# Narrower score products in a gated linear attention with a PReLU network: 80 and 112 columns instead of 128 and 116

## The chip, the cores and the metric

The kernel runs on one core of one Trainium2 chip. The metric is the device time of one execution in microseconds (us), the median of several runs; lower is better. A core has a matrix engine (TensorE, PE in the profile, with its weight loads shown apart as PEld), VectorE (DVE), ScalarE (ACT), GpSimd (POOL) and SyncE (SP), which here only issues DMAs. They run at the same time and wait for each other by semaphores. TensorE reads SBUF and writes PSUM; VectorE and ScalarE read both.

## The reference

Four sequences of 768 tokens, 8 heads of 48 channels, all in float32. Each head keeps a 48 x 48 state that is multiplied by a gate f, one value per channel, and takes in one outer product per token:

```python
f = 1.0 / (1.0 + np.exp(-f_logit))
for t in range(S):
    state = f[:, :, t, :, None] * state + np.einsum('bhd,bhe->bhde', k[:, :, t], v[:, :, t])
    y[:, :, t] = np.einsum('bhd,bhde->bhe', q[:, :, t], state)
```

The result goes as x, 3072 tokens of 384 channels, through a network with 2048 hidden channels and a slope per channel below zero:

```python
h = x @ w_in
g = np.maximum(h, 0.0) + alpha * np.minimum(h, 0.0)
return g @ w_out
```

## The kernel before

Tokens go in chunks of C = 128. A step handles U = 2 sequences of one chunk, so there are 12 steps. Heads lie in pairs, one at partitions 0 to 47 and one at 64 to 111 (`par`), four pairs to a sequence (`HP`). Inside a chunk the recurrence is a masked product of scores: token t takes from token s the sum over channels of q[t] times k[s] times all the gates after s up to t. The 128 x 128 scores are built from blocks of DB = 32 tokens, and each diagonal block from quads of 4 tokens (NB = 8 quads to a block). Inside a quad the gates between s and t are few, and they are multiplied into q: `qd` holds q with the products of d gates, for d = 0 to 3. Between quads the kernel multiplies k by the gates to the end of its quad (`k4`), and q by the gates from the beginning of its own quad and of the m - 1 quads between (`us`).

Preparing a step (VectorE and ScalarE; cut). W is 1024 tokens' columns (2 sequences x 4 pairs x 128), G = 32 blocks:

```python
qd = const.tile([128, 4 * (W + 1)], F32, tag="qd", name="qd")
for d in range(1, 4):                       # what no lag reaches is zeroed once
    nc.gpsimd.memset(qd[:, d * W:(d + 1) * W].rearrange("p (n r) -> p n r", r=4)[:, :, 0:d], 0.0)
# ... per step:
nc.scalar.activation(f, f, AF.Sigmoid)
nc.scalar.copy(kr[:, :, 2:3], f[:, :, 3:4])
qdv = [qd[:, d * W:(d + 1) * W] for d in range(4)]
nc.scalar.copy(qdv[0], q)
def lagged(d):
    nc.vector.tensor_tensor(quads(qdv[d])[:, :, d:4], quads(qdv[d - 1])[:, :, d:4],
                            f[:, :, 1:5 - d], ALU.mult)
# ... lagged(1), lagged(2), lagged(3) between products of f; then:
q4 = us[:, :, 0:DB].rearrange("p g (i r) -> p g i r", r=4)
skew = qd.rearrange("p (r x) -> p r x", r=4)[:, :, 0:W].rearrange("p r (n four) -> p n r four", four=4)
nc.scalar.copy(q4, skew[:, :, :, 0].rearrange("p (g i) r -> p g i r", i=NB))
# ... two scans, then q4 *= first gate of each quad, and us for the further quads: earlier(2) to earlier(7)
```

The gather takes row r of each quad from lag r, at a stride. The scores of one sequence (`attend`), two products and their evictions into the diagonal blocks `ad`:

```python
for u in range(U):
    raw = pair(f"raw{u}_{i}")               # one of 2 PSUM buffers of two banks
    for hp in range(HP):
        for j in range(NJ):
            g = (u * HP + hp) * C + j * DB
            for par in range(2):
                r_ = rows(par)
                nc.tensor.matmul(raw[DB * j:DB * (j + 1), par, hp * C:(hp + 1) * C],
                                 lhsT=k[r_, g:g + DB],
                                 rhs=qd[r_, 0:4 * W].rearrange("p (d x) -> p d x", d=4)[:, :, g:g + DB],
                                 start=True, stop=True)
    for d in range(4):
        nc.vector.copy_predicated(adu, mraw[:, d]..., rv[:, :, d])      # 128 x 256
    qu = pair(f"qu{u}_{i}")
    # the same loops: matmul(qu[..., hp * UW:(hp + 1) * UW], lhsT=k4[...], rhs=us[r_, g])   UW = 116
    for m in range(1, NB):
        nc.vector.copy_predicated(ad[:, u, :, :, 4 * m:DB], mquad..., qu...)   # 224, 192, ... 32
    yield
for u in range(U):
    # four ScalarE copies of ad into A
    yield
# py: the scores A (and the incoming state) times v; yield
# the state moved on (VectorE), y copied (ScalarE), xT[...] <- y by 10 DMAs; yield
```

So every 32 x 32 diagonal block is multiplied with all four lags: 4 x 32 = 128 columns. A float32 `matmul` shows as two MATMUL and two LDWEIGHTS records.

`carry` makes the products between blocks (`off`), a transpose (`pk`) and the new state (`pd`). `network` is the second half, in 12 pieces: eight of `ph` = x times w_in for two groups of 128 hidden channels, each with a ScalarE and two VectorE instructions that give `g`, and four of `po` = g times w_out. The pieces of neighbouring steps are interleaved by strings in which P and Q stand for pieces of prepare (of this and of the next step), O of carry, S of attend, n of the network of the step before, and a, w, b, v for pieces of loading the two weights, which are unpacked on the chip in the first steps:

```python
first = ("P3 a P a2 w P O a w3 S a P w S O a Q a S3 w a w S w Q a", ...)      # the first four steps
usual = "O n4 S n S Q n Q O n S2 n Q n Q S n S n Q n Q"
```

Each engine takes its instructions in the order in which the program issues them.

Of the kernel before, what the change touches and what calls it, by code (L numbers as in the profile page):

```python
# [8 lines left out]
F32 = mybir.dt.float32  # L9
# [3 lines left out]
I32 = mybir.dt.int32  # L13
U32 = mybir.dt.uint32
AF = mybir.ActivationFunctionType
ALU = mybir.AluOpType

C = 128
DB = 32
# [5 lines left out]
NB = DB // 4  # L25
# [5 lines left out]
def kernel(  # L31
# [28 lines left out]
    nc = tc.nc  # L60
    B, NC, _, HP, _ = qT.shape
    DM = v.shape[-1]
    H = 2 * HP
# [5 lines left out]
    W = U * HP * C  # L69
    GC = W // CH  # L70
    G = W // DB
    NJ = C // DB
    UO = [0, 0]
    for m in range(1, NB):
        UO.append(UO[-1] + (DB if m == 1 else DB - 4 * m))
    UW = UO.pop()

    const = ctx.enter_context(tc.tile_pool(name="const", bufs=1))
    work = ctx.enter_context(tc.tile_pool(name="work", bufs=2))
# [3 lines left out]
    def pair(name):  # L83
        return psa.tile([128, 2, 512], F32, tag="pair", name=name)
# [17 lines left out]
    ones = const.tile([128, NS], F32, tag="ones", name="ones")  # L102
    nc.gpsimd.memset(ones, 0.0)
    nc.gpsimd.memset(ones[:, 0:NS:NB + 1], 1.0)
    qd = const.tile([128, 4 * (W + 1)], F32, tag="qd", name="qd")
    for d in range(1, 4):
        nc.gpsimd.memset(qd[:, d * W:(d + 1) * W].rearrange("p (n r) -> p n r", r=4)[:, :, 0:d], 0.0)
    nc.gpsimd.memset(qd[:, 4 * W:], 0.0)
    bias = const.tile([128, 2], F32, tag="bias", name="bias")
    nc.gpsimd.memset(bias[:, 0:1], -896.0 * 128)  # L110
    nc.gpsimd.memset(bias[:, 1:2], -(896.0 + 2048) * 128)
# [2 lines left out]
    mraw = const.tile([128, 4, NB, 4], F32, tag="mraw", name="mraw")  # L114
# [5 lines left out]
    nc.vector.tensor_reduce(inq, diag, mybir.AxisListType.X, ALU.add)  # L120
    mquad = const.tile([128, UW], F32, tag="mquad", name="mquad")
    nc.gpsimd.memset(mquad, 0.0)
    for m in range(1, NB):
        lo = UO[m] + (4 if m == 1 else 0)
        n = NB - m
        nc.gpsimd.tensor_copy(mquad[:, lo:lo + 4 * n].rearrange("p (i r) -> p i r", r=4),
                              inq[:, 0:n].unsqueeze(2).broadcast_to((128, n, 4)))
    ad = const.tile([128, U, 2, HP, DB], F32, tag="ad", name="ad")
# [82 lines left out]
    def rows(par):  # L211
        return slice(64 * par, 64 * par + D)

    def quads(t):
        return t.rearrange("p (n r) -> p n r", r=4)
# [12 lines left out]
    def prepare(bp, c, x):  # L228

        i = f"{bp}_{c}"  # L230
# [3 lines left out]
        def load(name, src, bufs=2):  # L234
            t = work.tile([128, W], F32, tag=name, name=f"{name}_{i}", bufs=bufs)
            loads.dma_start(out=t.rearrange("p (u x) -> p u x", u=U),  # L236
                              in_=src[b0:b0 + U, c].rearrange("u p h t -> p u (h t)"))
            return t

        f = quads(load("f", fT, 1))  # L240
        q = load("q", qT, 1)
        k = x["k"] = load("k", kT, 1)
# [5 lines left out]

        nc.scalar.activation(f, f, AF.Sigmoid)
        nc.scalar.copy(kr[:, :, 2:3], f[:, :, 3:4])  # L250
        qdv = [qd[:, d * W:(d + 1) * W] for d in range(4)]
        nc.scalar.copy(qdv[0], q)  # L252
        fq = fs[:, 0:NS - 1].rearrange("p (g i) -> p g i", i=NB + 1)[:, :, 1:NB + 1]
        by32 = "p (g i) r -> p g (i r)"

        def lagged(d):
            nc.vector.tensor_tensor(quads(qdv[d])[:, :, d:4], quads(qdv[d - 1])[:, :, d:4],  # L257
                                    f[:, :, 1:5 - d], ALU.mult)

        nc.vector.tensor_tensor(kr[:, :, 1:2], f[:, :, 2:3], f[:, :, 3:4], ALU.mult)  # L260
        lagged(1)
        nc.vector.tensor_tensor(kr[:, :, 0:1], f[:, :, 1:2], kr[:, :, 1:2], ALU.mult)
        lagged(2)
        nc.vector.tensor_tensor(fq, f[:, :, 0:1].rearrange(by32, i=NB), kr[:, :, 0:1].rearrange(by32, i=NB), ALU.mult)
        lagged(3)
        yield

        ps = work.tile([128, NS], F32, tag="ps", name=f"ps_{i}", bufs=1)  # L270
        us = x["us"] = work.tile([128, G, UW], F32, tag="us", name=f"us_{i}", bufs=1)
        q4 = us[:, :, 0:DB].rearrange("p g (i r) -> p g i r", r=4)
        skew = qd.rearrange("p (r x) -> p r x", r=4)[:, :, 0:W].rearrange("p r (n four) -> p n r four", four=4)
        nc.scalar.copy(q4, skew[:, :, :, 0].rearrange("p (g i) r -> p g i r", i=NB))  # L274
        nc.vector.tensor_tensor_scan(ps, fs, ones, 0.0, ALU.mult, ALU.add)
        ss = work.tile([128, NS], F32, tag="ss", name=f"ss_{i}", bufs=1)
        nc.vector.tensor_tensor_scan(ss[:, ::-1], fs[:, ::-1], ones[:, ::-1], 0.0, ALU.mult, ALU.add)
# [15 lines left out]
        k4 = x["k4"] = work.tile([128, W], F32, tag="k4", name=f"k4_{i}", bufs=1)  # L293
# [108 lines left out]
    def attend(bp, c, x):  # L402

        i = f"{bp}_{c}"
        k, k4, us = (x[n] for n in ("k", "k4", "us"))


        for u in range(U):
            raw = pair(f"raw{u}_{i}")
            for hp in range(HP):  # L410
                for j in range(NJ):
                    g = (u * HP + hp) * C + j * DB
                    for par in range(2):
                        r_ = rows(par)
                        nc.tensor.matmul(raw[DB * j:DB * (j + 1), par, hp * C:(hp + 1) * C],  # L415
                                         lhsT=k[r_, g:g + DB],
                                         rhs=qd[r_, 0:4 * W].rearrange("p (d x) -> p d x", d=4)[:, :, g:g + DB],
                                         start=True, stop=True)
            adu = ad[:, u].rearrange("p r h t -> p (r h) t")
            rv = raw.rearrange("p r (h d t) -> p (r h) d t", h=HP, d=4)  # L420
            for d in range(4):
                nc.vector.copy_predicated(  # L422
                    adu, mraw[:, d].rearrange("p i r -> p (i r)").bitcast(I32).unsqueeze(1).broadcast_to((128, H, DB)),
                    rv[:, :, d])
            qu = pair(f"qu{u}_{i}")
            for hp in range(HP):
                for j in range(NJ):
                    g = (u * HP + hp) * NJ + j
                    for par in range(2):
                        r_ = rows(par)  # L430
                        nc.tensor.matmul(qu[DB * j:DB * (j + 1), par, hp * UW:(hp + 1) * UW],  # L431
                                         lhsT=k4[r_, g * DB:(g + 1) * DB], rhs=us[r_, g], start=True, stop=True)
            for m in range(1, NB):
                lo = UO[m] + (4 if m == 1 else 0)
                n = DB - 4 * m
                nc.vector.copy_predicated(  # L436
                    ad[:, u, :, :, 4 * m:DB],
                    mquad[:, lo:lo + n].bitcast(I32).unsqueeze(1).unsqueeze(1).broadcast_to((128, 2, HP, n)),
                    qu[:, :, 0:HP * UW].rearrange("p r (h x) -> p r h x", h=HP)[:, :, :, lo:lo + n])
# [4 lines that stand above are left out]
                s_ = slice(DB * j, DB * (j + 1))  # L444
                nc.scalar.copy(A[s_, u, :, s_], ad[s_, u].rearrange("p r h t -> p (r h) t"))  # L445
            yield


        py = pair(f"py_{i}")
        for u in range(U):  # L450
            for hp in range(HP):
                for cc in range(NC2):
                    for par in range(2):
                        hd = 2 * hp + par
                        o = hp * C + CH * cc
                        nc.tensor.matmul(py[64 * par:64 * par + 64, u, o:o + CH],  # L456
                                         lhsT=vs[bp][:, cc, u, hd * D:hd * D + 64],
                                         rhs=A[:, u, par * HP + hp, CH * cc:CH * (cc + 1)],
                                         start=True, stop=True)
        yield  # L460
        if c < NC - 1:
            x["moved"](1)
        y = work.tile([128, U, HP, C], F32, tag="ksn", name=f"y_{i}", bufs=1)
        for u in range(U):
            nc.scalar.copy(y[:, u].rearrange("p h t -> p (h t)"), py[:, u])
        xT = x["T"] = work.tile([128, NK, T], F32, tag="xT", name=f"xT_{i}")
        for hd in range(H):
            d = hd * D
            while d < (hd + 1) * D:
                n = min((hd + 1) * D, (d // 128 + 1) * 128) - d  # L470
                p0 = 64 * (hd % 2) + d - hd * D
                (nc.sync if hd % 2 else nc.scalar).dma_start(
                    out=xT[d % 128:d % 128 + n, d // 128].rearrange("p (u t) -> p u t", u=U),
                    in_=y[p0:p0 + n, :, hd // 2])
                d += n
        yield

    def network(bp, c, x):
# [37 lines left out]

    steps = [(bp, c) for c in range(NC) for bp in range(B // U)]
    first = (
# [4 lines left out]
    )  # L523
    usual = "O n4 S n S Q n Q O n S2 n Q n Q S n S n Q n Q"
    pieces = {key: part for keys, parts in (("aw", load_weights(w_in_sb, w_in, "w_in")),
                                            ("bv", load_weights(w_out_sb, w_out, "w_out")))
              for key, part in zip(keys, parts)}
# [74 lines left out]
```

## Time and profile before

| what | value |
|---|---|
| time, median of 3 runs | 670.87 us (670.18 to 671.96) |
| span of the profiled run | 670.8 us, 17033 instructions |
| mean granted TensorE clock | 0.994 |
| PE / PEld / DVE / ACT busy | 626.8 / 465.9 / 419.8 / 263.8 us |
| raw: PE busy, mean of one record | 29.4 us, 286 ns (1536 records) |
| qu: PE busy, mean of one record | 27.5 us, 274 ns (1536 records) |
| eviction of raw, DVE | 42.5 us, 443 ns (96) |
| gather into us, ACT | 24.7 us, 2059 ns (12) |

How to read it: a line of a group gives the line of the code, the engine, the operation, output <- inputs, shape and count; then the busy time, the mean time of one, and the idle time of the engine just before it, with what ended that. The chain of waits is followed back from the last instruction, at each step to what released it. Records of small matmuls overlap, so a group's busy time is less than count times mean.

### The profile page before, as it was taken

How to read it: one execution, taken by the hardware profiler on the slowest of the kernel's cores; microseconds unless marked ns; L12 is line 12 of the kernel's file. 1: busy time of each engine (PE TensorE's matmuls, PEld its weight loads, DVE VectorE, ACT ScalarE, POOL GpSimd, SP SyncE). 2: the span in 40 equal slices, each digit the busy share in tenths (PEclk: the TensorE clock that was granted, in tenths of full speed). 3: DMA queues.
4: the chain of work that ended last, by engine and by line, in shares of the span. 5: the costliest groups of instructions: out<-in, count | busy, mean ns of one | idle time of the engine just before them, and what ended most of it. 6: DMA issues, size and time to landing. Idle time of an engine off the chain costs nothing.

```text
span 670.8 us, 17033 instructions
## 1 busy us (share of the span) xinstructions
PE 626.8 (93%) x7392; PEld 465.9 (69%) x7392; DVE 419.8 (63%) x897; ACT 263.8 (39%) x457; POOL 70.8 (11%) x113
## 2 busy tenths in 40 slices
PE   0558899999999999999999999999999999999997
PEld 0446766876876876875876876876876786786774
DVE  5899889692675486486387397297298197170120
ACT  5755794443152441451450450451441442421110
POOL 8232232010000001001001001001001000000000
PEclk9998899999999999999999999999999999999999
DMA  6878996212112023023022023023023010000000
GB/s 230 268 199 273 264 247 166 60 40 69 34 64 72 3 64 87 18 64 79 26 64 79 25 65 79 24 64 79 25 64 80 25 34 24 24 3 24 24 0 23
DMA packets 29129, 53.03 MB, mean 79 GB/s; under 512 B 4320, under 2 KB 16864, under 8 KB 29056
## 3 DMA queue, kind: packets, MB, share of 16 engines
q0 software_dynamic: 9616, 27.92, 15.1%
q1 hardware_dynamic: 13584, 21.63, 10.3%
q10 hardware_dynamic: 5856, 2.40, 1.5%
q8 instruction: 58, 0.95, 0.6%
q14 instruction: 15, 0.12, 0.1%
HBM read 36.21 MB, written 4.72 MB: 61 GB/s over the span
## 4 chain that ended last, share of the span: by engine, by line
PE 82%; DVE 9%; ACT 3%; DMA 3%; issue 2%; ACTq 0%; DVEq 0%; SPq 0%
PE po L502 34%; PE ph L486 34%; PE py L456 4%; PE raw L415 3%; PE qu L431 3%; PE pk L368 2%; DVE ad L436 2%; DMA xT<-y 2%; PE pd L380 2%; DVE ad L422 2%; ACT us L274 1%; PE off L355 1%; DVE us L288 1%; DMA w_out_raw<-in_w_out 1%; DVE g L494 1%
## 5 line engine op out<-in xcount | busy, mean ns | idle before, releaser
L486 PE MATMUL ph<-xT,w_in_sb 128*128 128x256 f32 x1152 | 265.6, 388 | 7.5 <-DMA xT<-y 7.5
L502 PE MATMUL po<-w_out_sb,g 128*128 128x384 f32 x768 | 252.9, 488 | 0.2 <-DVE g L494 0.2
L486 PEld LDWEIGHTS ph<-xT,w_in_sb 128*128 128x128 f32 x1152 | 219.0, 193 | 42.5 <-DMA w_in_sb<-w_in_lead 6.9
L502 PEld LDWEIGHTS po<-w_out_sb,g 128*128 128x128 f32 x768 | 144.8, 190 | 97.7 <-ACT neg L491 0.8
L494 DVE SCALAR_TENSOR_TENSOR g<-neg,om,ph 128x256 f32<-128x256 f32 x192 | 83.3, 476 | 202.3 <-ACT neg L491 201.9
L491 ACT ACTIVATE neg<-ph 128x512 f32<-128x512 f32 x96 | 57.1, 597 | 140.4 <-PE ph L486 132.4
L508 ACT COPY o<-po 128x384 f32<-128x384 f32 x24 | 11.5, 479 | 156.7 <-PE po L502 156.7
L436 DVE COPY_PREDICATED ad<-mquad,qu 128x224 f32<-128x224 int32 (+6 forms) x168 | 50.4, 300 | 8.4 <-DVE ad L422 0.5
L288 DVE TENSOR_TENSOR us<-us,fs 128x768 f32<-128x768 f32 (+2 forms) x72 | 44.5, 617 | 0.2
L422 DVE COPY_PREDICATED ad<-mraw,raw 128x256 f32<-128x256 int32 x96 | 42.5, 443 | 2.7
L274 ACT COPY us<-qd 128x1024 f32<-128x1024 f32 x12 | 24.7, 2059 | 40.0 <-DVE qd L257 35.3
L445 ACT COPY A<-ad 32x256 f32<-32x256 f32 x96 | 38.4, 400 | 2.3 <-DVE ad L436 0.9
L236 POOL DMA_DIRECT2D k<-in_kT x11 | 8.0, 731 | 272.1 <-PE raw L415 239.2
L431 PE MATMUL qu<-us,k 48*32 48x116 f32 x1536 | 27.5, 274 | 5.2 <-DVE us L288 2.3
L339 ACT COPY A<-q 48x512 f32<-48x512 f32 x48 | 29.6, 617 | 5.7 <-DVE f L334 4.1
L415 PE MATMUL raw<-qd,k 48*32 48x128 f32 x1536 | 29.4, 286 | 2.4 <-DVE ad L422 2.4
L456 PEld LDWEIGHTS py<-A,vs 128*64 128x64 f32 x768 | 25.1, 145 | 7.2 <-ACT neg L491 3.3
L415 PEld LDWEIGHTS raw<-qd,k 48*32 48x32 f32 x1536 | 22.6, 110 | 10.4 <-issue 10.4
L355 PE MATMUL off<-q,kh 48*32 48x32 f32 x768 | 9.4, 199 | 20.7 <-DVE q L306 20.0
L257 DVE TENSOR_TENSOR qd<-qd,f 128x768 f32<-128x768 f32 (+2 forms) x36 | 27.1, 752 | 2.0 <-ACT qd L252 2.0
L431 PEld LDWEIGHTS qu<-us,k 48*32 48x32 f32 x1536 | 22.5, 109 | 8.3 <-PE raw L415 5.7
L456 PE MATMUL py<-A,vs 128*64 128x64 f32 x768 | 26.9, 231 | 0.9 <-DVE vs L396 0.7
(66 smaller groups left out, 442.5 us busy)
## 6 DMA issues: line engine op xcount, KB each, us to landing
w_in_raw<-in_w_in SPq DMA_DIRECT2D x12, 511.8 KB, 6.2
w_out_raw<-in_w_out SPq DMA_DIRECT2D x12, 511.8 KB, 5.3
f<-in_fT POOLq DMA_DIRECT2D x11, 512.0 KB, 4.4
q<-in_qT POOLq DMA_DIRECT2D x11, 512.0 KB, 5.1
k<-in_kT POOLq DMA_DIRECT2D x11, 512.0 KB, 4.0
out<-o SPq DMA_DIRECT2D x24, 192.0 KB, 1.9
vs<-in_v POOLq DMA_DIRECT2D x22, 192.0 KB, 4.6
w_in_sb<-w_in_lead POOLq DMA_DIRECT2D x12, 256.0 KB, 5.8
```

Source lines behind the costliest of these rows:

```text
L274: nc.scalar.copy(q4, skew[:, :, :, 0].rearrange("p (g i) r -> p g i r", i=NB))
L288: nc.vector.tensor_tensor(us[:, :, UO[m]:UO[m] + 4 * n].rearrange("p g (i r) -> p g i r", r=4), us[:, :, skip:skip + 4 * n].rearrange("p g ...
L415: nc.tensor.matmul(raw[DB * j:DB * (j + 1), par, hp * C:(hp + 1) * C], lhsT=k[r_, g:g + DB], rhs=qd[r_, 0:4 * W].rearrange("p (d x) -> p d ...
L422: nc.vector.copy_predicated(adu, mraw[:, d].rearrange("p i r -> p (i r)").bitcast(I32).unsqueeze(1).broadcast_to((128, H, DB)), rv[:, :, d])
L431: nc.tensor.matmul(qu[DB * j:DB * (j + 1), par, hp * UW:(hp + 1) * UW], lhsT=k4[r_, g * DB:(g + 1) * DB], rhs=us[r_, g], start=True, stop= ...
L436: nc.vector.copy_predicated(ad[:, u, :, :, 4 * m:DB], mquad[:, lo:lo + n].bitcast(I32).unsqueeze(1).unsqueeze(1).broadcast_to((128, 2, HP, ...
L445: nc.scalar.copy(A[s_, u, :, s_], ad[s_, u].rearrange("p r h t -> p (r h) t"))
L456: nc.tensor.matmul(py[64 * par:64 * par + 64, u, o:o + CH], lhsT=vs[bp][:, cc, u, hd * D:hd * D + 64], rhs=A[:, u, par * HP + hp, CH * cc: ...
L486: nc.tensor.matmul(ph[:, j * T:(j + 1) * T], lhsT=w_in_sb[:, kt, (f + j) * 128:(f + j + 1) * 128], rhs=xT[:, kt], start=(kt == 0), stop=(k ...
L491: nc.scalar.activation(neg, phv, AF.Relu, scale=-1.0)
L494: nc.vector.scalar_tensor_tensor(g[:, j], neg[:, j], om[:, f + j:f + j + 1], phv[:, j], ALU.mult, ALU.add)
L502: nc.tensor.matmul(po[u][:, 0:DM], lhsT=gs[f // 2][:, f % 2, u * C:(u + 1) * C], rhs=w_out_sb[:, f], start=(f == 0), stop=(f == NF - 1))
```

## The change

The first product needs, for lag d, only those tokens that have d predecessors in their quad: 4 - d of 4. A mask throws the others away. The change stores `qd` by block, with the lags packed side by side (32 + 24 + 16 + 8 = 80 columns), so that one matmul streams 80 columns that lie together. The eviction of lag d then reads and writes 8 x 8 x (4 - d) elements per partition instead of 8 x 32. The second product leaves out the first 4 of its 116 columns, which no mask selects either. The zeroing of `qd` falls away; the gather, which used one stride through all lags, becomes four copies. The strings of the order are written anew.

```diff
+    QO = [0]
+    for d in range(4):
+        QO.append(QO[-1] + NB * (4 - d))
+    QW = QO.pop()
 ...
-    qd = const.tile([128, 4 * (W + 1)], F32, tag="qd", name="qd")
-    for d in range(1, 4):
-        nc.gpsimd.memset(qd[:, d * W:(d + 1) * W].rearrange("p (n r) -> p n r", r=4)[:, :, 0:d], 0.0)
-    nc.gpsimd.memset(qd[:, 4 * W:], 0.0)
+    qd = const.tile([128, G, QW], F32, tag="qd", name="qd")
 ...
-        qdv = [qd[:, d * W:(d + 1) * W] for d in range(4)]
-        nc.scalar.copy(qdv[0], q)
+        qdv = [qd[:, :, QO[d]:QO[d] + NB * (4 - d)].rearrange("p g (i r) -> p g i r", r=4 - d) for d in range(4)]
+        nc.scalar.copy(qd[:, :, 0:DB], q.rearrange("p (g t) -> p g t", t=DB))
 ...
-            nc.vector.tensor_tensor(quads(qdv[d])[:, :, d:4], quads(qdv[d - 1])[:, :, d:4],
-                                    f[:, :, 1:5 - d], ALU.mult)
+            nc.vector.tensor_tensor(qdv[d], qdv[d - 1][:, :, :, 1:5 - d],
+                                    f[:, :, 1:5 - d].rearrange("p (g i) r -> p g i r", i=NB), ALU.mult)
 ...
-        nc.scalar.copy(q4, skew[:, :, :, 0].rearrange("p (g i) r -> p g i r", i=NB))
+        for r in range(4):
+            nc.scalar.copy(q4[:, :, :, r], qdv[r][:, :, :, 0])
 ...
-                        nc.tensor.matmul(raw[DB * j:DB * (j + 1), par, hp * C:(hp + 1) * C],
-                                         lhsT=k[r_, g:g + DB],
-                                         rhs=qd[r_, 0:4 * W].rearrange("p (d x) -> p d x", d=4)[:, :, g:g + DB],
-                                         start=True, stop=True)
+                        nc.tensor.matmul(raw[DB * j:DB * (j + 1), par, hp * C:hp * C + QW],
+                                         lhsT=k[r_, g * DB:(g + 1) * DB], rhs=qd[r_, g], start=True, stop=True)
 ...
             for d in range(4):
+                n = 4 - d
                 nc.vector.copy_predicated(
-                    adu, mraw[:, d].rearrange("p i r -> p (i r)").bitcast(I32).unsqueeze(1).broadcast_to((128, H, DB)),
-                    rv[:, :, d])
+                    adu[:, :, :, d:4], mraw[:, d, :, d:4].bitcast(I32).unsqueeze(1).broadcast_to((128, H, NB, n)),
+                    rv[:, :, QO[d]:QO[d] + NB * n].rearrange("p h (i t) -> p h i t", t=n))
 ...
-                        nc.tensor.matmul(qu[DB * j:DB * (j + 1), par, hp * UW:(hp + 1) * UW],
-                                         lhsT=k4[r_, g * DB:(g + 1) * DB], rhs=us[r_, g], start=True, stop=True)
+                        nc.tensor.matmul(qu[DB * j:DB * (j + 1), par, hp * UW + 4:(hp + 1) * UW],
+                                         lhsT=k4[r_, g * DB:(g + 1) * DB], rhs=us[r_, g, 4:UW], start=True, stop=True)
 ...
     first = (
-        "P3 a P a2 w P O a w3 S a P w S O a Q a S3 w a w S w Q a",
-        "a P a w P a w P w n2 w b v w S b2 v n b v n O v n S b S v b n v O b v S P n b n v n2 S b v Q b v n b2 v Q v2 Q3 S n Q",
-        "n2 O n S n S Q n O Q S n Q n2 S n S Q2 n S n Q n",
-        "O n S n S n4 Q n2 S Q2 O S Q n2 S n S n Q2",
+        "P2 a2 P2 w a2 w P O w P a w S2 O w Q S2 a w a S a S Q w2",
+        "a P w a w a P w n P a n w b v w S b v n b n O v b v n b v S P S n b O b v n b S v2 n2 S n b v Q b v b n v b v2 Q3 S n Q",
+        "n2 O n S n2 S Q S n S O n2 Q n Q2 n P S n S Q n Q",
+        "n S n2 S Q n2 O n S n S Q n O Q2 n Q S2 Q n3",
     )
-    usual = "O n4 S n S Q n Q O n S2 n Q n Q S n S n Q n Q"
+    usual = "O n2 S n2 S2 n O n Q n Q n S n2 S Q n S Q2 n Q"
```

More of the change, by code (lines that the diff above doesn't have):

```diff
@@ L272, in prepare @@
         q4 = us[:, :, 0:DB].rearrange("p g (i r) -> p g i r", r=4)
-        skew = qd.rearrange("p (r x) -> p r x", r=4)[:, :, 0:W].rearrange("p r (n four) -> p n r four", four=4)
-        nc.scalar.copy(q4, skew[:, :, :, 0].rearrange("p (g i) r -> p g i r", i=NB))
+        for r in range(4):
+            nc.scalar.copy(q4[:, :, :, r], qdv[r][:, :, :, 0])
         nc.vector.tensor_tensor_scan(ps, fs, ones, 0.0, ALU.mult, ALU.add)
@@ L411, in attend @@
                 for j in range(NJ):
-                    g = (u * HP + hp) * C + j * DB
+                    g = (u * HP + hp) * NJ + j
                     for par in range(2):
                         r_ = rows(par)
-                        nc.tensor.matmul(raw[DB * j:DB * (j + 1), par, hp * C:(hp + 1) * C],
-                                         lhsT=k[r_, g:g + DB],
-                                         rhs=qd[r_, 0:4 * W].rearrange("p (d x) -> p d x", d=4)[:, :, g:g + DB],
-                                         start=True, stop=True)
-            adu = ad[:, u].rearrange("p r h t -> p (r h) t")
-            rv = raw.rearrange("p r (h d t) -> p (r h) d t", h=HP, d=4)
+                        nc.tensor.matmul(raw[DB * j:DB * (j + 1), par, hp * C:hp * C + QW],
+                                         lhsT=k[r_, g * DB:(g + 1) * DB], rhs=qd[r_, g], start=True, stop=True)
+            adu = ad[:, u].rearrange("p r h (i t) -> p (r h) i t", t=4)
+            rv = raw.rearrange("p r (h x) -> p (r h) x", h=HP)
             for d in range(4):
+                n = 4 - d
                 nc.vector.copy_predicated(
-                    adu, mraw[:, d].rearrange("p i r -> p (i r)").bitcast(I32).unsqueeze(1).broadcast_to((128, H, DB)),
-                    rv[:, :, d])
+                    adu[:, :, :, d:4], mraw[:, d, :, d:4].bitcast(I32).unsqueeze(1).broadcast_to((128, H, NB, n)),
+                    rv[:, :, QO[d]:QO[d] + NB * n].rearrange("p h (i t) -> p h i t", t=n))
             qu = pair(f"qu{u}_{i}")
```

## The prediction, made before the changed kernel was run

> **What bounds the kernel now.** I read the page's first part, then busy time by stretch, then the chain of waits, then the timeline of one period, then the counts of matmuls begun in 100 ns steps, and last the groups kept apart by shape.
>
> ```profile
> PE 626.8 (93%) x7392; PEld 465.9 (69%) x7392; DVE 419.8 (63%) x897; ACT 263.8 (39%) x457; POOL 70.8 (11%) x113
> ```
>
> TensorE (PE) is busy 93% of the span; VectorE (DVE) and ScalarE (ACT) have room on average. By stretch (us; then length; busy us of PE, weight loads, DVE, ACT, POOL; clock; DMA share; GB/s):
>
> ```profile
> 0.00:45.00 45.00, 16.46 (x456) 14.29 (x456) 34.36 (x75) 28.42 (x44) 22.15 (x47) 1.00 0.73 232
> 66.00:113.00 47.00, 43.74 (x457) 31.34 (x456) 42.89 (x97) 30.86 (x52) 15.48 (x19) 0.96 0.92 243
> 216.05:267.24 51.19, 51.03 (x624) 37.91 (x627) 33.27 (x70) 19.17 (x34) 3.37 (x5) 1.00 0.19 56
> ```
>
> So there are two kernels. From about 113 us on each step takes 51.2 us and PE fills all of it. Before that PE idles, DVE is 34.4 of 45 and 42.9 of 47 us busy, and the DMA engines are 0.73 to 0.92 busy with the weights. In the chain of waits (start, length, what) the score stages of one period stand on the path:
>
> ```profile
> 228.12 1.09 PE raw L415 x64
> 229.21 0.81 PE qu L431 x59
> ...
> 232.81 1.12 PE raw L415 x64
> 234.06 1.09 PE qu L431 x61
> ```
>
> The timeline says why the second pair is longer:
>
> ```profile
> 231.60 2.31 DVE L436 COPY_PREDICATED ad<-mquad,qu 128x224 f32<-128x224 int32 x7
> 234.03 0.87 PEld L431 LDWEIGHTS qu<-us,k 48*32 48x32 f32 x64 [0.40 <-PE raw L415]
> ```
>
> The qu of u=1 takes the PSUM buffer of the qu of u=0 (two buffers, raw and qu in turn), which VectorE reads until 231.60 + 2.31 = 233.91; qu starts at 234.03. The label blames raw; the time fits the eviction. Raw u=0 to the next ph takes 228.05 to 229.95 = 1.90 us, u=1 232.74 to 235.07 = 2.33 us: 0.43 us of wait in each period.
>
> How fast does PE begin these matmuls? Counts begun so far (first x), 128 columns, then 116, then the 32 columns of off:
>
> ```profile
> 228.00:228.20 0.20, 0.15 (x10) 0.15 (x18) 1.00 0.00 0
> 228.00:228.90 0.90, 0.85 (x61) 0.85 (x64) 1.00 0.00 0
> ```
> ```profile
> 228.70:229.00 0.30, 0.05 (x4) 0.11 (x10) 1.00 0.00 0
> 228.70:229.70 1.00, 0.75 (x60) 0.81 (x64) 1.00 0.00 0
> ```
> ```profile
> 215.90:216.00 0.10, 0.02 (x3) 0.02 (x3) 1.00 0.00 0
> 215.90:216.50 0.60, 0.52 (x60) 0.52 (x62) 1.00 0.00 0
> ```
>
> Raw: 51 in 0.70 us, 13.7 ns each. Qu: 56 in 0.70 us, 12.5 ns. Off: 57 in 0.50 us, 8.8 ns. From 128 to 116 columns the step is 0.10 ns per column; carried on to 32 columns it would give 4.1 ns, so a floor of about 8.8 ns stops it.
>
> **The Trainium skill.** "TensorEngine Tiling (Array Packing)", Available Configurations, lists 64x32 tiles as 8 independent ones. The trace agrees: ph streams 256 columns in 2.79 us / 12 = 232 ns, so 128 columns take 116 ns; over 8 tiles that is 14.5 ns, against 13.7 measured. "TensorE: Matmul & The Clock Gate", in the section on 56 ns against 53.3 ns, says that starts never come closer than about 25 ns however few the columns. A floor exists here, but at 8.8 ns with eight tiles in flight; the measurement decides. "ScalarE: Activation LUTs", What ACT_TABLE_LOAD costs, gives 186 ns plus 0.833 ns per element: 1039 ns for 1024, and the plain copy of q takes 1049. The strided gather of 1024 takes 2059, so the page does not hold for a stride of four floats.
>
> **The change part by part.** Groups by shape (busy us, mean ns):
>
> ```profile
> L422 DVE COPY_PREDICATED ad<-mraw,raw 128x256 f32<-128x256 int32 x96 | 42.5, 443 | 2.7
> L436 DVE COPY_PREDICATED ad<-mquad,qu 128x192 f32<-128x192 int32 x24 | 8.9, 370 | 0.9
> L436 DVE COPY_PREDICATED ad<-mquad,qu 128x128 f32<-128x128 int32 x24 | 7.2, 300 | 0.9
> L436 DVE COPY_PREDICATED ad<-mquad,qu 128x64 f32<-128x64 int32 x24 | 5.5, 229 | 0.9
> L250 ACT COPY kr<-f 128x256 f32<-128x256 f32 x12 | 8.3, 691 | 0.4
> L274 ACT COPY us<-qd 128x1024 f32<-128x1024 f32 x12 | 24.7, 2059 | 40.0 <-DVE qd L257 35.3 <-DVE w_in_sb L187 4.6
> ```
>
> 1. Raw at 80 columns. 80/128 of 13.7 is 8.6 ns, just under the floor. I take 9.3 ns, since two limits that meet seldom act as a clean maximum: 64 x (13.7 - 9.3) = 0.28 us per u, 0.56 us per step, all on the path in the steady part.
> 2. Qu at 112 columns: 4 x 0.10 ns x 64 = 0.03 us per u, 0.06 us per step.
> 3. Raw evictions: four of 256 elements become 256, 192, 128 and 64, whose durations the same instruction already shows: 4 x 443 = 1772 ns becomes 443 + 370 + 300 + 229 = 1342 ns. That is 0.43 us per u, 10.3 us of DVE over 24 u, beside PE in the steady part.
> 4. The usual order now puts two network stages (2 x 2.8 us) between the two score stages where one stood. With 5.6 us in between and an eviction of 0.43 us less, the 0.43 us wait of the second qu goes.
> 5. The gather into us: one ACT copy of 2059 ns becomes four of 256 elements at stride four, like kr's 691 ns: 2.8 us, so 0.7 us more ACT a step. ACT is busy 19 of 51 us, so nothing in the steady part. In step 0 the first three can run while VectorE still multiplies, and only the last, 0.7 us, is exposed: 1.4 us gained on the path.
> 6. Memsets of qd (2 us on POOL) end at 3.5 us, before f lands at 5.5 us: nothing.
>
> Steady sum: 0.56 + 0.06 + 0.43 = 1.05 us per step. Steps 2 to 11 run there: 10 x 1.05 = 10.5 us. Start: 1.4 us in step 0, plus 2 x 0.43 us of its evictions on the path, = 2.3 us; from these I keep 2, because the DMA engines are nearly full and later steps re-order work in ways I can't add up. 670.9 - 10.5 - 2 = 658.4 us.
>
> **The rivals.** (a) PE's issue, not the array, sets the score stages: raw and qu both show about 0.9 us for their 64 weight loads, with 128 and 116 columns. Then 80 columns save nothing and only the wait and the start remain: 670.9 - 4.3 - 2 = 664.6. Against it: off does its 64 loads in 0.65 us. (b) A new wait at the end of a step. py and the state update now come one po stage (5.2 us) later. Before:
>
> ```profile
> 300.66 2.08 PE L456 MATMUL py<-A,vs 128*64 128x64 f32 x64
> ...
> 312.44 0.71 DVE L334 TENSOR_TENSOR f<-ps 48x8 f32<-48x8 f32 x4
> ```
>
> After py the DVE still needs the state update (2.1 us) and two prepare stages (3.7 and 3.2 us): 9.0 us, and off, which needs them, comes 2 x 5.2 = 10.5 us after py. xT needs y's copy (1.1 us) and DMAs whose last issue is at 309.7, landing some 4 us later at most: 11 us after py, against 10.5 + 0.7 + 1.0 = 12.2 us. Both fit by only 1 to 1.5 us. If one misses by 1 us in ten steps, the time is about 668. (c) The start. Its order was rewritten for the first four steps; DVE and DMA both near full, it could give 5 us more or lose 5: 653 or 663.
>
> **Range and chances.** Centre 658.4; (a) lifts it by 6, (b) by up to 10, (c) moves it by 5 either way. I take 651 to 666 for 8 in 10. The limit of 2% lies at 657.5, just under the centre: faster by over 2% 0.42, within 2% 0.55, slower 0.03, which needs both a missed wait and a lost start.
>
> **What would show it.** Right: a steady step of 50.1 us instead of 51.2; raw starts about 9 ns apart; no idle PE before the second qu; the four raw evictions at 443, 370, 300, 229 ns; gathers of about 0.7 us. Step 1 is wrong if raw's 64 starts still take over 0.8 us; step 4 if a wait on VectorE stays before qu, or a new one stands before off or ph; the start is wrong if the first 113 us of work end more than 4 us off from 2 us sooner. The small last evictions (runs of one to three elements) could cost more than the evenly laid ones of the same count; that would show in DVE alone.

## The result, and the profile after

The changed kernel takes 659.73 us (median of 4 runs, 658.33 to 660.70) against 671.32 us before, a ratio of 0.983 (95% interval 0.980 to 0.985): 11.6 us less, where 12.5 us were predicted.

The page's first part and, under it, busy time in one steady step (columns as in the prediction):

```profile
PE 615.5 (93%) x7392; PEld 458.0 (70%) x7392; DVE 420.2 (64%) x897; ACT 267.0 (41%) x493; POOL 69.9 (11%) x109
```
```profile
261.15:311.49 50.34, 50.34 (x624) 37.48 (x627) 33.34 (x70) 19.42 (x37) 3.38 (x5) 1.00 0.20 56
```

A step takes 50.34 us instead of 51.19, and PE is busy in all of it. DVE's total is what it was, 420.2 against 419.8 us: first sign that the smaller evictions are not cheaper. The timeline of that step's score stages:

```profile
267.97 0.73 PEld L416 LDWEIGHTS raw<-qd,k 48*32 48x32 f32 x64 [0.33 <-issue]
268.67 1.07 PE L431 MATMUL qu<-us,k 48*32 48x112 f32 x64
269.50 1.86 DVE L422 COPY_PREDICATED ad<-mraw,raw 128x256 f32<-128x256 int32 x4
269.66 5.45 PE L486 MATMUL ph<-xT,w_in_sb 128*128 128x256 f32 x24
271.46 2.29 DVE L436 COPY_PREDICATED ad<-mquad,qu 128x224 f32<-128x224 int32 x7
275.04 0.92 PE L416 MATMUL raw<-qd,k 48*32 48x80 f32 x64
275.73 1.07 PE L431 MATMUL qu<-us,k 48*32 48x112 f32 x64
276.73 2.86 PE L486 MATMUL ph<-xT,w_in_sb 128*128 128x256 f32 x12
```

From raw to the next ph it is 269.66 - 267.97 = 1.69 us for u=0 (before 1.90) and 276.73 - 275.04 = 1.69 us for u=1 (before 2.33). The first qu's evictions end at 271.46 + 2.29 = 273.75, two microseconds ahead of the second qu, so nothing waits. But the four raw evictions still take 1.86 us. Counts of raw matmuls begun, and the groups by shape:

```profile
268.00:268.10 0.10, 0.10 (x14) 0.10 (x22) 1.00 0.00 0
268.00:268.60 0.60, 0.60 (x60) 0.60 (x64) 1.00 0.00 0
```
```profile
L422 DVE COPY_PREDICATED ad<-mraw,raw 128x192 f32<-128x192 int32 x24 | 10.7, 445 | 0.9
L422 DVE COPY_PREDICATED ad<-mraw,raw 128x128 f32<-128x128 int32 x24 | 10.6, 442 | 0.9
L422 DVE COPY_PREDICATED ad<-mraw,raw 128x64 f32<-128x64 int32 x24 | 10.6, 441 | 0.9
L422 DVE COPY_PREDICATED ad<-mraw,raw 128x256 f32<-128x256 int32 x24 | 10.4, 435 | 0.0
```

46 raw matmuls begin in 0.50 us, one every 10.9 ns (before 13.7, predicted 9.3). An eviction takes 435 to 445 ns, whether it has 256 elements or 64.

Where the 12.4 us between the two profiles lie: off of step 2 starts at 115.31 instead of 118.42 us (3.1 us); from there to off of step 4, 95.51 instead of 97.63 us (2.1 us); from there to the last network's start at 613.68, 402.86 instead of 410.01 us (7.2 us). The first of these is not all the change's: the profiled execution of before took 672.67 us, 1.35 more than the median, and in it the first load, f, landed late. Its sigmoid starts at 5.54 us, against 4.74 in the changed kernel's profile and 4.71 in that of the second run below, which has the loads and the `qd` of before. By the medians 11.6 - 2.1 - 7.2 = 2.3 us are left for the start.

### The profile page after: what moved, and what is told of

Read it like the earlier page. It is cut to its first block, busy times and chain, and to the rows that moved or that the text cites. A ratio compares the mean times of both kernels' runs of the same rounds, so it can differ in the third digit from the quotient of the medians.

```text
span 658.4 us, 17032 instructions
## 1 busy us (share of the span) xinstructions
PE 615.5 (93%) x7392; PEld 458.0 (70%) x7392; DVE 420.2 (64%) x897; ACT 267.0 (41%) x493; POOL 69.9 (11%) x109
## 4 chain that ended last, share of the span: by engine, by line
PE 84%; issue 7%; POOL 4%; DVE 2%; ACT 1%; DMA 1%; POOLq 0%
PE po L502 36%; PE ph L486 35%; PE py L456 3%; PE qu L431 3%; PE raw L416 3%; PE pk L369 2%; PE pd L381 2%; POOL w_in_sb L191 1%; PE off L356 1%; POOL w_out_sb L191 1%; DMA w_out_sb<-w_out_lead 1%; DVE us L289 0%; POOL vs L138 0%; ACT A L340 0%; POOL vs L247 0%
## 5 line engine op out<-in xcount | busy, mean ns | idle before, releaser
L465 ACT COPY y<-py 128x512 f32<-128x512 f32 x24 | 12.9, 591 | 81.2 <-PE py L456 81.2
L422 DVE COPY_PREDICATED ad<-mraw,raw 128x256 f32<-128x256 int32 (+1 forms) x96 | 42.3, 441 | 2.7
L391 DVE TENSOR_TENSOR vs<-vs,f 48x768 f32<-48x768 f32 x20 | 19.1, 953 | 30.4 <-PE py L456 30.0
L275 ACT COPY us<-qd 128x256 f32<-128x256 f32 x48 | 29.6, 666 | 12.2 <-DVE qd L258 7.4
L431 PE MATMUL qu<-us,k 48*32 48x112 f32 x1536 | 26.4, 265 | 2.6 <-DVE us L289 1.7
L416 PEld LDWEIGHTS raw<-qd,k 48*32 48x32 f32 x1536 | 18.1, 108 | 10.6 <-issue 10.2
```

Source lines behind the costliest of these rows:

```text
L275: nc.scalar.copy(q4[:, :, :, r], qdv[r][:, :, :, 0])
L416: nc.tensor.matmul(raw[DB * j:DB * (j + 1), par, hp * C:hp * C + QW], lhsT=k[r_, g * DB:(g + 1) * DB], rhs=qd[r_, g], start=True, stop=True)
L422: nc.vector.copy_predicated(adu[:, :, :, d:4], mraw[:, d, :, d:4].bitcast(I32).unsqueeze(1).broadcast_to((128, H, NB, n)), rv[:, :, QO[d]: ...
L431: nc.tensor.matmul(qu[DB * j:DB * (j + 1), par, hp * UW + 4:(hp + 1) * UW], lhsT=k4[r_, g * DB:(g + 1) * DB], rhs=us[r_, g, 4:UW], start=T ...
```

## The experiments

Theory A: the second qu waits for VectorE, and the narrower product is worth little unless that wait is moved out of its way. Rival B: the narrower product brings the gain, the new order is beside the point. The first two runs take the change apart.

**The changed kernel with the order of before**

```diff
-    usual = "O n2 S n2 S2 n O n Q n Q n S n2 S Q n S Q2 n Q"
+    usual = "O n4 S n S Q n Q O n S2 n Q n Q S n S n Q n Q"
     # and the four strings of first as before
```

> The changed kernel with the order strings of before. Theory A (the wait swallows it): the second qu cannot start before the evictions of the first qu end, some 5.85 us after the first raw starts, whatever raw costs; a steady step falls from 51.2 only to about 51.1 us, the 0.4 us of idle before the second qu becomes 0.6 us, and the time is 668 to 671 us (the start keeps 1 to 2 us of the shorter gather). Rival B (the columns do it): the step falls to about 50.4 us, time 660 to 663 us.

Measured: 670.66 us against 670.83, ratio 1.000 (0.999 to 1.002). A step takes 51.16 us (off at 213.30 and 264.46). Second raw and qu in its timeline:

```profile
228.84 2.31 DVE L436 COPY_PREDICATED ad<-mquad,qu 128x224 f32<-128x224 int32 x7
229.77 0.92 PE L416 MATMUL raw<-qd,k 48*32 48x80 f32 x64
...
231.29 1.07 PE L431 MATMUL qu<-us,k 48*32 48x112 f32 x64 [0.60 <-DVE ad L436]
```

The evictions end at 231.15 and qu starts at 231.29. It waits longer than before, because all else became faster; now the profile itself names the eviction. B falls: under the old order the narrower products bring nothing that the times show.

**The kernel before with the new order**

The four strings of first and `usual` as in the change, all else as before.

> The kernel before (128 and 116 columns, one gather) with the order strings of the change. Theory A: only the wait of 0.43 us goes, a steady step of about 50.75 us, and the start gains what its new order is worth, 1 to 4 us; time 663 to 667 us. Rival B: the order is worth nothing in the steady part, step 51.1 to 51.2 us, time 668 to 671 us.

Measured: 664.54 us, ratio 0.991 (0.989 to 0.993). A step takes 50.76 us (the chain of waits at two successive off), 0.43 less, the wait of the prediction:

```profile
211.46 0.69 PE off L355 x50
262.22 0.69 PE off L355 x50
```

The order alone brings 6.3 us, just over half of the gain. With the columns the step falls on from 50.76 to 50.34, which over ten steps is 4.2 of the 5.3 us that are left; the remaining 1.1 us are within the noise of the two ratios.

**The old order with the evictions shortened**

To see the wait from its other end: the order of before, and the evictions made short.

```diff
-            for d in range(4):
+            for d in range(1):      # lags 1 to 3 of the first product are left out
                 n = 4 - d
                 nc.vector.copy_predicated(
```

> The changed kernel with the order strings of before, and only lag 0 of the first product evicted (lags 1 to 3 are left out, so the result is not the reference's). If the old order loses because the second qu waits for the evictions of the first, taking 1.33 us of them away ends the wait with nothing moved: no idle before the second qu, a step of 50.3 to 50.4 us instead of 51.16. If the old order costs by itself (more switches, later loads), the step stays at 51.1.

Measured: 658.15 us, ratio 0.980 (0.978 to 0.982), step 50.33 us (off at 208.54 and 258.87):

```profile
222.65 2.30 DVE L436 COPY_PREDICATED ad<-mquad,qu 128x224 f32<-128x224 int32 x7
225.01 0.92 PE L416 MATMUL raw<-qd,k 48*32 48x80 f32 x64
225.71 1.07 PE L431 MATMUL qu<-us,k 48*32 48x112 f32 x64
```

The evictions end at 224.95, just ahead of the second raw, and qu follows raw after 0.70 us without idle. In the steady steps the old order costs nothing by itself; what it cost was this wait. A stands.

**Why the evictions stayed at 441 ns**

Two runs reshape them.

```diff
 # e3, last three evictions: mask of lag 1 packed; lag 2 on half the quads; lag 3 in runs of 16
+ copy_predicated(adu[:, :, :, 1:4], mpk..., raw...)                          # 192, runs of 3
+ copy_predicated(adu[:, :, 0:4, 2:4], mraw[:, 2, 0:4, 2:4]..., raw...)       # 64, 32 runs of 2
+ copy_predicated(ad[...][:, :, 0:16], mpk..., raw...)                        # 128, runs of 16
```

> The changed kernel with its last three raw evictions reshaped (lag 2 and 3 then write other scores, so the result is not the reference's): lag 1 the same 192 elements with the mask packed without gaps; lag 2 only half the quads, 64 elements in 32 runs of 2; lag 3 128 elements in 8 runs of 16. Theory C (each short run of the output costs as much as four elements): 192 elements stay at about 440 ns, 64 in 32 runs take about 300 ns, 128 in runs of 16 take 300 ns. Rival D (the gaps in the mask do it): lag 1 falls to about 370 ns. Rival E (a fixed floor of the four-dimensional form): 64 elements in 32 runs stay at about 440 ns.

```profile
L438 DVE COPY_PREDICATED ad<-mpk,raw 128x192 f32<-128x192 int32 x24 | 10.7, 445 | 0.9
...
L438 DVE COPY_PREDICATED ad<-mpk,raw 128x128 f32<-128x128 int32 x24 | 7.1, 295 | 0.8
L438 DVE COPY_PREDICATED ad<-mraw,raw 128x64 f32<-128x64 int32 x24 | 7.1, 295 | 0.8
```

A packed mask changes nothing (D falls), 64 elements in 32 runs cost as much as 128 without gaps (E falls): each run of two was paid as four.

```diff
 # e8, last three: output in runs of 5, three apart; only the PSUM source with gaps; only the mask with gaps
+ copy_predicated(full.rearrange("p g (i t) -> p g i t", t=8)[:, :, :, 0:5], ..., ...)     # 160
+ copy_predicated(full[:, :, 0:16]..., ..., rv[...][:, :, :, 0:2])                         # 128
+ copy_predicated(full[:, :, 0:8]..., mraw[:, 0, :, 0:1]..., rv[:, :, 72:80]...)           # 64
```

> The changed kernel with its raw evictions of lags 1 to 3 reshaped (they write other scores, so the result is not the reference's). Lag 1: 160 elements in runs of 5 with gaps of 3. Lag 2: 128 elements, output and mask without gaps, the source in PSUM in runs of 2 four apart. Lag 3: 64 elements, output and source without gaps, the mask with a stride of four. Theory (a run of n elements costs as the next multiple of four, whatever operand has the gap): 160 take 441 ns, 128 take 441 ns, 64 take 441 ns. If only gaps of the output count: 441, 300, 229 ns. If runs shorter than four cost four and longer ones cost their length: 160 take 334 ns.

```profile
L424 DVE COPY_PREDICATED ad<-mraw,raw 128x160 f32<-128x160 int32 x24 | 10.7, 445 | 0.8
...
L428 DVE COPY_PREDICATED ad<-mraw,raw 128x128 f32<-128x128 int32 x24 | 7.1, 296 | 0.8
L432 DVE COPY_PREDICATED ad<-mraw,raw 128x64 f32<-128x64 int32 x24 | 6.4, 268 | 0.8
```

Runs of 5 are paid as 8. Gaps in the PSUM source are free; gaps in the mask alone cost 268 instead of 229 ns. So it is the output, nearly the second of the three outcomes: it is paid by groups of four floats touched. (Every run here begins at a group's start or lies inside one group, so a rule that rounds each run up to a multiple of four fits as well; the runs do not tell the two apart.) It is not paid by the stretch it spans: the evictions of qu write 4 of every 32 columns in 194 ns. All four lags touch the same 64 groups, hence about 441 ns each.

**How the product's time falls with its columns**

```diff
-    rhs=qd[r_, g]
+    rhs=qdf[r_, g * QW:g * QW + COLS[bp][u]]     # 48, 64, 96, 112; evictions read what was written
```

> The changed kernel with 48, 64, 96 and 112 columns in the first product, by sequence of the step (wrong or missing columns, so the result is not the reference's); the 64 starts of a raw are counted. Theory F (a floor and the array meet softly): 48 columns 9 to 9.6 ns between starts, 64 about 10, 96 about 11.5, 112 about 12.2. Rival G (a clean maximum of a floor of 10.9 ns and the array): 48 and 64 stay at 10.9, 96 about 10.9, 112 about 12.

The 64 weight loads of raw at 96 and at 48 columns (start, length first), from the timeline:

```profile
265.95 0.78 PEld L419 LDWEIGHTS raw<-qd,k 48*32 48x32 f32 x64 [0.33 <-issue]
...
316.44 0.67 PEld L419 LDWEIGHTS raw<-qd,k 48*32 48x32 f32 x64 [0.33 <-issue]
```

The same at 64 and 112 columns takes 0.70 and 0.83 us, at 80 columns in the changed kernel 0.73, at 128 in the one before 0.89: from 48 to 128 columns 0.67, 0.70, 0.73, 0.78, 0.83, 0.89 us. There is no knee: the rise per 16 columns grows slowly, from 0.03 to 0.06 us (G falls). Counted as starts, 48 columns give 53 in 0.50 us (9.4 ns), 64 give 49 in 0.50 us (10.2 ns), 96 give 49 in 0.60 us (12.2 ns), 112 give 48 in 0.60 us (12.5 ns). F holds to within 0.7 ns. Going from 80 to 64 columns would save 0.03 us more for each raw, an estimate from these spans.

**The first four steps**

The changed kernel with the old `first` and the new `usual`.

> The changed kernel with the order of before in its first four steps and the new one after. Steady step 50.3 us as in the changed kernel. If the rewritten first four steps are worth 3 us or so, the time is 662 to 664 us; if the start gains from the gather alone and its order is worth nothing, 659.5 to 660.5 us.

Measured: 664.04 against 671.37 us, ratio 0.989 (0.987 to 0.992), with steady steps of 50.33 us. Against 0.983 for the change, the rewritten first four steps are worth about 0.66% or 4.4 us (2 to 7, from the two intervals). Two of the steps are steady ones, where the old order has its wait: the second qu starts 1.52 and 1.47 us after its raw instead of 0.69, together about 1.6 us. Some 2.8 us belong to the start, hardly more than the uncertainty.

No run points to a version that is better than the change and still computes the reference: those with a lower median or single time leave scores out or write others.

## Why the prediction was right

The time lies 1.3 us from the centre. The wait was read rightly, but the steady sum was too large, and the start came out near its 2 us for other reasons than those given; that the total is so near is partly luck.

- **Step 1, raw at 80 columns: right in kind, too large.** 9.3 ns between starts was taken, 10.9 measured: 64 x (13.7 - 10.9) = 0.18 us per u instead of 0.28. The reasoning failed where it took 8.8 ns for a floor and let the time fall in step with the columns almost down to it; the column run shows one slow curve from 48 to 128.
- **Step 2, qu at 112 columns:** 12.2 ns measured (49 starts in 0.60 us) against 12.1 expected: 0.02 us per u.
- **Step 3, the evictions: wrong.** 1342 ns was expected for four, 1763 measured (435 + 445 + 442 + 441), as before. Durations were taken from evictions of the same element count whose output lies in whole groups of four. The prediction named this danger and rightly placed it in VectorE alone. The steady part did not feel it, since the new order took the wait away by itself.
- **Step 4, the wait: right.** 0.43 us predicted; the order alone lowers a step by 51.19 - 50.76 = 0.43 us. But it was listed as one saving beside others. It was the condition for the others: under the old order the narrower product is worth 0.03 us a step, under the new one 0.42 us.
- **Step 5, the gather: cost right, gain too large.** The four copies take 666 ns each (mean in the groups by shape), against 691 expected. (The 2059 ns of the old gather was put down to a stride of four floats. In the code its innermost step, from row to row, is W + 1 = 1025 floats; the copy with a stride of four on both sides is that of kr.) The 1.4 us were ScalarE's saving, but while the old gather ran VectorE had two scans to do and waited for only 0.86 us of it. Before:

```profile
13.59 1.23 DVE L279 TENSOR_TENSOR us<-us,f 128x1024 f32<-128x1024 f32 x1 [0.86 <-ACT us L274]
```

  In the second run, with the old gather and f landing as early as in the changed kernel's profile, this product starts at 12.79 us; in the changed kernel it starts at 11.84, 0.95 us sooner. That this reaches the end is not shown: with the old order of the first steps the medians differ from before by 0.2 us and, beyond the steady steps' 8 x 0.85 = 6.8 us, by 0.5 us, both less than the runs of one kernel scatter.
- **The sum.** Steady: 2 x (0.18 + 0.02) + 0.43 = 0.83 us a step against 0.85 measured and 1.05 predicted; over ten steps 2.1 + 7.2 = 9.3 us measured instead of 10.5. Start: 2.3 us by the medians instead of 2. The order alone, with the old gather and evictions, gives 6.3 - 10 x 0.43 = 2.0 us there. The prediction had put the order at nothing, with 5 us either way, and added up a gather and evictions, of which the evictions gave nothing and the gather nothing that the times show.
- **Rivals.** (a) was partly true: the gain per column shrinks below 128, yet it does not vanish. (b) did not come, and its margin was wider than reckoned: off needs only kh and the first of the two q products from us, not all of both prepare stages. In step 0 off starts at 18.28 us, right after that product's end at 18.23 and before the other. In a steady step py ends at 300.90, the product ends at 306.25 and off starts at 311.42, so 5.2 us were to spare, not 1.5. (c) came out on the good side, by 2 to 3 us (2.0 here, 2.8 by the run on the first four steps).

## What to carry to other kernels

A stage on the busiest engine is shortened in vain if its successor waits for a buffer that another engine empties: compare the end of the eviction with the next start before counting columns, and move other work in between first. A saving on one engine counts on the path only as far as the others wait for it. Price an instruction by one with the same access pattern, not by one with the same element count. The time of many small matmuls on separate tiles fell here much more slowly than their columns.

## What the runs showed of the hardware

- A predicated copy of float32 to SBUF was paid by groups of four output floats touched: runs of 1, 2 and 3 cost as 4, runs of 5 as 8 (435 to 445 ns for 64 groups, 295 for 32). VectorE's product of two tensors showed no such rounding: before the change the lags were written in runs of 3 and 2 with gaps, in 950 ns for 768 elements and 684 for 512; only in single elements it was dear, 624 ns for 256.
- The weight loads of 64 pairs of weight load and matmul on eight tiles of 64 x 32 take 0.67 us at 48 columns and 0.89 us at 128: 2.7 times the columns for 1.33 times the time.
- A ScalarE copy of 256 floats that writes at a stride of four took 666 ns; the four copies read at strides of 4, 3, 2 and 1 and took 0.68, 0.67, 0.65 and 0.64 us in step 0, so the reading stride hardly mattered. The same number 32 partitions wide into runs of 32 took 400 ns.
- The TensorE clock granted in the first 66 us differed between profiles, from 0.77 in the changed kernel's to 0.97 in that before, without a mark on the start: two runs of the changed kernel with the old first steps, at 0.95 and 0.79, reach off of step 2 at 115.70 and 115.71 us.
- Single executions of the kernel before ranged from 668.43 to 672.35 us in one set of 23, so a start that differs by 2 or 3 us between two single profiles proves little; the medians decide.
